# Moving columns of the fp32r matmuls taken alternately from two places 2048 bytes apart

## The chip, the cores and the metric

One core of one Trainium2 chip runs the program. The metric is the device time of one execution in microseconds, taken as the median of 3 runs.

## The reference, cut to what matters

`x` is 8 x 3072 x 256 in float32, `w_in` 256 x 2048, `w_out` 2048 x 256.

```python
X = np.fft.fft(x, axis=1)          # 3072 tokens
X = np.fft.fft(X, axis=2).real     # 256 features
h = X.reshape(8 * 3072, 256) @ w_in
g = h * np.tanh(softplus(h))       # the Mish function
out = g @ w_out
```

## The kernel before, in words

**Chunks.** The host writes the input in an order that lets symmetric tokens be added and subtracted, so that a batch (8 of them) becomes 3 chunks. A chunk has two matrices of 128 x 512, P (cosine part) and Q (sine part): its column c stands for two tokens, t and 3072 - t, whose hidden values are P-part + Q-part and P-part - Q-part. `CHUNK_TOKENS` says which token stands in which column, and `_slots` tells the host from which chunk and place of the output a token is fetched: token t from column c, its mirror from column 512 + c.

**Three-term products.** Each large product is made of three matmuls in fp32r, a type with which one matmul is one pass: a value is split into a high part, rounded to fp32r (ScalarE, `A.copy`), and the low part that is left. `split_to` (L468) does it for P and Q: ScalarE makes `ph` or `qh` (L470), VectorE or GpSimd `pl` or `ql` (L471). The matmuls of the token transform (L452 to L459) are in plain fp32, each of which appears in the trace as two records, with a weight load each. Each of the four parts of a chunk is a tile of 128 x 512 of its own, of which there are two (`new_chunk`, L463, pool `pq` with 2 buffers).

**The main loop** has 390 turns `tau`, 384 of which make a step s = tau: 8 batches x 3 chunks x 16 blocks `f` of 128 hidden units. A turn issues, in this order:

- `mm1(tau)` (L827 to L829): 6 matmuls with 512 moving columns each, 3 with `ph`, `pl`, `ph` into the PSUM tile `pa` and 3 with `qh`, `ql`, `qh` into `pb`;
- `mm2(tau - 6)` (L857): 12 matmuls with 512 moving columns each into four PSUM accumulators (2 halves of the output features x 2 halves of the 1024 token columns), from `gh` and `gl`;
- `make_h` on VectorE (L836 to L838): `h` = `pa` plus the zero-frequency row `p0b` times `wc0`, then plus `pb` into columns 0 to 511 and minus `pb` into columns 512 to 1023 of a slot of `hring`;
- `split(tau - 4)`: ScalarE casts `h` to `gh` (L846), GpSimd makes `gl` (L847; in the first 12 steps VectorE);
- the Mish activation on ScalarE (L945), in place;
- pieces of other work, given by hand: `EARLY` for the first 19 turns (conversion of the float64 weights, the first batch's sums), and after that the next batch's sums on VectorE and GpSimd (`fold_ops`, turns 10 to 44 of a batch), the transforms of `first_chunk` (turns 44 and 45), `other_chunks` (turns 1, 2, 5 and 7; in the first batch 12 to 15) and the splits of `last_chunk` (turns 17 and 18).

So 18 matmuls with 512 moving columns run in each turn, one after the other, with neighbouring columns 4 bytes apart in SBUF:

```python
T.matmul(dst, wh[:, fs], q[n + "h"], start=True, stop=False)
T.matmul(acc[i], w[:, f, 128 * d:128 * d + 128], g[:, 512 * t:512 * t + 512], **kw)
```

Before the loop, `cs` (the feature transform's table, used by `make_wc`, last in turn 10) lies in a buffer of the tag `ql`, and the small tile of `make_mids` in one of the tag `pl`. `first_p0` (L717), `col_z` (L678) and `col_cs` write the zero-frequency rows with 8 or 128 partitions. Near the end `single_h` (L900 to L902) and `single_out` (L918 to L920) compute one left-over token per batch, with 48 matmuls each; those of `single_out` have weights of only 8 columns and 256 moving columns in fp32r.

Of the kernel before, what the change touches and what calls it, by code (L numbers as in the profile page):

```python
# [10 lines left out]
F32 = mybir.dt.float32  # L11
F32R = mybir.dt.float32r
# [35 lines left out]
def _slots():  # L48

    chunk, place = np.zeros(S, np.int64), np.zeros(S, np.int64)  # L50
    for ch in range(3):
        for c, t in enumerate(CHUNK_TOKENS[ch]):
            chunk[t], place[t] = ch, c
            if t:
                chunk[S - t], place[S - t] = ch, 512 + c
    return chunk, place


# [215 lines left out]
def fft_moe(ctx, tc, x, col_d, mids_d, w_in, w_out, cs_d, dft_d, ysel_d, eye_d, out, single_d):  # L274
# [52 lines left out]
    xt = small(128, 12 * NB).rearrange("p (k c q b) -> p k c q b", k=2, c=2, q=3)  # L327
    xm = small(1, 6 * NB).rearrange("p (k q b) -> p k q b", k=2, q=3)
    eye = small(128, 128)
    cs = pqp.tile([128, 2, 2, 128], F32, tag="ql", name="cs")  # L330

    p0_d = dp.tile([NB, 3, 512], F32, name="p0_d")
    pe_d = dp.tile([NB, 1], F32, name="pe_d")
# [128 lines left out]

    def new_chunk(ch):  # L463
        q = {}
        for n in ("ph", "pl", "qh", "ql"):
            q[n] = pqp.tile([128, 512], F32R, tag=n, name=n)
        chunks[ch] = q

    def split_to(hi, lo, src, eng):
        A.copy(hi, src)  # L470
        eng.tensor_tensor(lo, src, hi, op=ALU.subtract)  # L471
# [11 lines left out]
    def first_chunk(b, par, part=(0, 1, 2)):  # L483

        ch = 3 * b
        st = folds[b]
        n = NE if par == 0 else 256
        sl = slice(256 * par, 256 * par + 256)
        if 0 in part:
            st["ps", par] = ps("pa"), ps("pb")  # L490
        pa, pb = st["ps", par]
        halves = [c for c in (0, 1) if c in part]
        transform(pa[:, :n], lambda c: fold_part(b, c, "e", 0, par), par, 0, None, halves)
        transform(pb[:, :n], lambda c: fold_part(b, c, "o", 0, par), par, 1, None, halves)
        if 2 in part:
            if par == 0:
                new_chunk(ch)
            q = chunks[ch]
            if par == 0:
                base = fp.tile([128, NE + 14], F32, tag="base", name="base")[:, :NE]  # L500
                add_mid(base, pa, 0, b)
                pa = base
            split_to(q["ph"][:, sl], q["pl"][:, sl], pa[:, :256], V)
            split_to(q["qh"][:, sl], q["ql"][:, sl], pb[:, :256], V)
            if par == 0:
                V.tensor_copy(ends[:, b:b + 1], pa[:, 256:257])

    def other_chunks(b, par, odd):

        ch = 3 * b + 1  # L510
        if par == 0 and not odd:
            new_chunk(ch)
            for o in range(2):
                full2[o] = fp.tile([128, 512], F32, tag=f"full{o}", name=f"full{o}")
        st = folds[b]
        n = NE if par == 0 else 256
        sl = slice(256 * par, 256 * par + 256)
        pa, pb = ps("pa"), ps("pb")
        y, cos, sin = ("o", 2, 1) if odd else ("e", 1, 2)
        transform(pa[:, :n], lambda c: fold_part(b, c, y, cos, par), par, 0)  # L520
        transform(pb[:, :n], lambda c: fold_part(b, c, y, sin, par), par, 1)

        base = fp.tile([128, NE + 14], F32, tag="base", name="base")[:, :NE]
        spare = fp.tile([128, 256], F32, tag="spare", name="spare")
        if par == 0:
            add_mid(base, pa, 1 + odd, b)
        else:
            V.tensor_copy(base[:, :n], pa[:, :n])

        scaled, plain = (base, pb) if odd else (pb, base)  # L530
        V.scalar_tensor_tensor(spare, scaled[:, :256], R3 if odd else -R3, plain[:, :256], op0=ALU.mult, op1=ALU.add)
        q = chunks[ch]
        h, l = ("qh", "ql") if odd else ("ph", "pl")
        split_to(q[h][:, sl], q[l][:, sl], spare, G)
        V.scalar_tensor_tensor(full2[odd][:, sl].rearrange("p (a s) -> p a s", s=128), later(scaled, par),
                               -R3 if odd else R3, later(plain, par), op0=ALU.mult, op1=ALU.add)

    def last_chunk(b, odd):

        ch = 3 * b + 2  # L540
        if not odd:
            new_chunk(ch)
        q = chunks[ch]
        h, l = ("qh", "ql") if odd else ("ph", "pl")
        split_to(q[h], q[l], full2[odd], G)

    p0b = {}

# [76 lines left out]
    sp = {}  # L625

    def make_mids():
        w = pqp.tile([128, 512], F32, tag="pl", name="mids")
        eo = w[:12 * NB, :256]
        V.tensor_tensor(eo[:, 0:128], ymid[:, 0:128], ymid[:, 128:256], op=ALU.add)  # L630
        V.tensor_tensor(eo[:, 128:256], ymid[:, 0:128], ymid[:, 128:256], op=ALU.subtract)
        n = 6 * NB
        ev, od = eo[:, 0:128], eo[:, 128:256]
        pa, pb = ps("pa"), ps("pb")
        T.matmul(pa[:n, 0:128], ysel[:, 0:n], ev, start=True, stop=True)
        T.matmul(pa[0:1, 128:128 + n], ymid[:, 256:257], ysel[:, 0:n], start=True, stop=True)
        T.matmul(pb[:n, 0:128], ysel[:, n:2 * n], od, start=True, stop=True)

        for i, (o, v) in enumerate(((n + NB, od), (n + 4 * NB, od), (3 * NB, ev))):
            T.matmul(pb[0:1, 128 * i + 128:128 * i + 256], ysel[:, o:o + 1], v, start=True, stop=True)  # L640
        m = w[:n, 256:]
        A.copy(m[:, 0:128], pa[:n, 0:128])
        A.copy(m[:, 128:256], pb[:n, 0:128])
        A.copy(xm, pa[0:1, 128:128 + n].rearrange("p (k q b) -> p k q b", k=2, q=3))
        A.copy(mid0, pb[0:1, 128:512])
        pc = psacc.tile([128, 512], F32, tag="acc0", name="pc")
        T.matmul(pc[:, 0:2 * NB], ev, ysel[:, 0:2 * NB], start=True, stop=True)
        T.matmul(pc[:, 2 * NB:3 * NB], od, ysel[:, n:n + NB], start=True, stop=True)
        A.copy(midc, pc[:, :3 * NB].rearrange("p (q b) -> p q b", b=NB))
        SP.dma_start(out=mid_d, in_=m)  # L650
# [20 lines left out]
    def col_z(par):  # L671
        n = NE if par == 0 else 256
        if par == 0:
            sp["z"] = p2.tile([128, 512], F32, tag="p0b", name="p0z")
        r = sp["z"][:NB]
        pa = ps("pa")
        transform(pa[:NB, :n], lambda c: xt[:, par, c, 0], par, 0, xm[:, 0, 0] if par == 0 else None)
        A.copy(r[:, 256 * par:256 * par + 256], pa[:NB, :256])  # L678
        if par == 0:
            A.copy(pe, pa[:NB, 256:257])  # L680
            SP.dma_start(out=pe_d, in_=pe)
            SP.dma_start(out=ends0, in_=bass.AP(pe_d.tensor, pe_d.offset, [[0, 128], [1, NB]]))
        else:
            SP.dma_start(out=p0_d[:, 0, :], in_=r)

    def col_cs(par):

        n = NE if par == 0 else 256
        if par == 0:
            sp["c"] = fp.tile([128, NE], F32, tag="full0", name="p0c")[:NB]  # L690
            sp[1] = fp.tile([128, 512], F32, tag="full1", name="p0d")[:NB]
            sp[2] = p2.tile([128, 512], F32, tag="p0b", name="p0o")[:NB]
        pa, pb = ps("pa"), ps("pb")
        transform(pa[:NB, :n], lambda c: xt[:, par, c, 1], par, 0, xm[:, 0, 1] if par == 0 else None)
        transform(pb[:NB, :n], lambda c: xt[:, 1 - par, c, 2], par, 1)
        A.copy(sp["c"][:, :n], pa[:NB, :n])
        for k in (1, 2):
            view = (lambda v: later(v, 1)) if k == 1 else (lambda v: later(v, par))
            V.scalar_tensor_tensor(later(sp[k][:, 256 * par:256 * par + 256], 1), view(pb[:NB]), R3 if k == 2 else -R3,
                                   view(sp["c"]), op0=ALU.mult, op1=ALU.add)  # L700
            if par:
                SP.dma_start(out=p0_d[:, k, :], in_=sp[k])

    def first_p0():
# [9 lines left out]
        for c in range(2):  # L714
            T.matmul(pa[:, 256:512], all_rows(xt[:, 1, c, 0]), const(c, 1, 0), start=c == 0, stop=c == 1)
        p0b[0] = p2.tile([128, 512], F32, tag="p0b", name="p0b")
        A.copy(p0b[0], pa)  # L717


    G.memset(alt, 0.0)  # L720
# [100 lines left out]
    def mm1(s):  # L821
        ch, f = divmod(s, NF)
        q = chunks[ch]
        fs = slice(128 * f, 128 * f + 128)
        pa, pb = ps("pa"), ps("pb")
        for dst, wh, wl, n in ((pa, wch, wcl, "p"), (pb, wsh, wsl, "q")):
            T.matmul(dst, wh[:, fs], q[n + "h"], start=True, stop=False)  # L827
            T.matmul(dst, wh[:, fs], q[n + "l"], start=False, stop=False)  # L828
            T.matmul(dst, wl[:, fs], q[n + "h"], start=False, stop=True)  # L829
        return pa, pb  # L830

    def make_h(s, pab):
# [16 lines left out]
    def mm2(s):  # L849
# [4 lines left out]

        def part(i, w, g, **kw):
            d, t = divmod(i, 2)
            T.matmul(acc[i], w[:, f, 128 * d:128 * d + 128], g[:, 512 * t:512 * t + 512], **kw)  # L857

        def high(i):
            part(i, woh, gh, start=f == 0, stop=False)  # L860
# [142 lines left out]
```

## Time and profile before

| | |
|---|---|
| median of 3 runs | 1746.48 us (1746.38 to 1746.68) |
| span of the profiled execution, first to last instruction | 1742.7 us |
| mean granted TensorE clock | 0.987 of full speed |
| instructions | 20578 |
| DMA, mean over the span | 39 GB/s |

The profile is of one execution. No time of its own is given for that execution beside its span; the runs' median is 3.8 us above the span, which is what lies before the first and after the last instruction. Busy time of TensorE (PE) is counted with modelled ends of pipelined matmuls, so that neighbouring matmuls overlap in it: how long a matmul really takes in a row of matmuls is read from the distance between starts. A timeline line gives the start, the duration, the engine, the line of the kernel, the operation with its output and inputs, and in brackets how long the engine was idle before it and what released it.

### The profile page before, as it was taken

How to read it: one execution, taken by the hardware profiler on the slowest of the kernel's cores; microseconds unless marked ns; L12 is line 12 of the kernel's file. 1: busy time of each engine (PE TensorE's matmuls, PEld its weight loads, DVE VectorE, ACT ScalarE, POOL GpSimd, SP SyncE). 2: the span in 40 equal slices, each digit the busy share in tenths (PEclk: the TensorE clock that was granted, in tenths of full speed). 3: DMA queues.
4: the chain of work that ended last, by engine and by line, in shares of the span. 5: the costliest groups of instructions: out<-in, count | busy, mean ns of one | idle time of the engine just before them, and what ended most of it. 6: DMA issues, size and time to landing. Idle time of an engine off the chain costs nothing.

```text
span 1742.7 us, 20578 instructions
## 1 busy us (share of the span) xinstructions
PE 1705.6 (98%) x7534; PEld 1397.0 (80%) x7534; DVE 1117.7 (64%) x1680; ACT 864.3 (50%) x968; POOL 1163.3 (67%) x654
## 2 busy tenths in 40 slices
PE   7788999999999999999999999999999999999999
PEld 4466888888888888888888888888888888888887
DVE  7997775566755666566755666556666667554453
ACT  3445454554544554455545545445544555454454
POOL 1456885687756876587756877568765777554555
PEclk8889999999999999999999999999999999998999
DMA  4212000200020000200002000100002000000000
GB/s 178 85 43 80 24 25 7 103 31 0 31 78 26 30 25 7 103 1 31 25 7 103 31 1 31 64 40 31 25 7 103 1 31 25 7 31 13 19 25 24
DMA packets 25375, 67.57 MB, mean 39 GB/s; under 512 B 3141, under 2 KB 3618, under 8 KB 25274
## 3 DMA queue, kind: packets, MB, share of 16 engines
q1 hardware_dynamic: 24474, 64.91, 10.4%
q8 instruction: 59, 0.97, 0.2%
q10 hardware_dynamic: 800, 1.35, 0.2%
q14 instruction: 42, 0.34, 0.1%
HBM read 40.97 MB, written 25.27 MB: 38 GB/s over the span
## 4 chain that ended last, share of the span: by engine, by line
PE 93%; DVE 5%; POOL 0%; issue 0%; ACT 0%; DMA 0%; ACTq 0%; DVEq 0%
PE acc L857 59%; PE pa L827 5%; PE pa L828 5%; PE pb L828 5%; PE pa L829 5%; PE pb L827 5%; PE pb L829 5%; PE pb L452 1%; PE pa L452 1%; DVE hring L836 1%; DVE gl L847 1%; DVE hring L837 1%; DVE hring L838 0%; PE pb L455 0%; DVE xring L579 0%
## 5 line engine op out<-in xcount | busy, mean ns | idle before, releaser
L847 POOL TENSOR_TENSOR gl<-hring,gh 128x1024 fp32r<-128x1024 f32 x372 | 896.7, 2411 | 475.4 <-ACT gh L846 474.8
L846 ACT CAST gh<-hring 128x1024 fp32r<-128x1024 f32 x384 | 403.1, 1050 | 733.1 <-PE acc L857 701.0
L857 PE MATMUL acc<-gh,wol 128*128 128x512 f32 x1536 | 600.8, 391 | 1.8 <-POOL wol L622 1.8
L857 PE MATMUL acc<-gh,woh 128*128 128x512 f32 x1536 | 600.9, 391 | 0.4 <-ACT woh L621 0.4
L836 DVE SCALAR_TENSOR_TENSOR hring<-p0b,wc,pa 128x512 f32<-128x512 f32 x384 | 286.5, 746 | 437.9 <-PE pa L829 422.6
L857 PE MATMUL acc<-gl,woh 128*128 128x512 f32 x1536 | 422.7, 389 | 0.0
L945 ACT ACTIVATE hring<-hring 128x1024 f32<-128x1024 f32 x384 | 404.4, 1053 | 33.4 <-DVE hring L838 24.6
L857 PEld LDWEIGHTS acc<-gh,wol 128*128 128x128 f32 x1536 | 290.3, 189 | 63.2 <-POOL wol L622 2.6
L857 PEld LDWEIGHTS acc<-gh,woh 128*128 128x128 f32 x1536 | 290.4, 189 | 61.5 <-ACT woh L621 0.9
L857 PEld LDWEIGHTS acc<-gl,woh 128*128 128x128 f32 x1536 | 289.1, 188 | 60.4
L837 DVE TENSOR_TENSOR hring<-hring,pb 128x512 f32<-128x512 f32 x384 | 264.0, 688 | 42.7 <-DVE hring L836 1.8
L838 DVE TENSOR_TENSOR hring<-hring,pb 128x512 f32<-128x512 f32 x384 | 263.8, 687 | 13.3
L827 PE MATMUL pa<-ph,wch 128*128 128x512 f32 x384 | 158.9, 414 | 9.0 <-DVE hring L836 6.8
L827 PE MATMUL pb<-qh,wsh 128*128 128x512 f32 x384 | 151.2, 394 | 4.4 <-ACT qh L470 3.3
L828 PE MATMUL pa<-pl,wch 128*128 128x512 f32 x384 | 151.0, 393 | 0.0
L828 PE MATMUL pb<-ql,wsh 128*128 128x512 f32 x384 | 150.5, 392 | 0.3 <-POOL ql L471 0.3
L829 PE MATMUL pa<-ph,wcl 128*128 128x512 f32 x384 | 150.7, 392 | 0.0
L829 PE MATMUL pb<-qh,wsl 128*128 128x512 f32 x384 | 150.6, 392 | 0.0
L827 PEld LDWEIGHTS pa<-ph,wch 128*128 128x128 f32 x384 | 72.6, 189 | 25.6 <-DVE hring L836 7.8
L827 PEld LDWEIGHTS pb<-qh,wsh 128*128 128x128 f32 x384 | 72.8, 189 | 22.1 <-ACT qh L470 3.7
L829 PEld LDWEIGHTS pa<-ph,wcl 128*128 128x128 f32 x384 | 72.9, 190 | 15.4
L828 PEld LDWEIGHTS pb<-ql,wsh 128*128 128x128 f32 x384 | 72.7, 189 | 15.8 <-POOL ql L471 0.6
(259 smaller groups left out, 1143.9 us busy)
## 6 DMA issues: line engine op xcount, KB each, us to landing
xring<-x_dram SPq DMA_DIRECT2D x32, 768.0 KB
out_dram<-ot SPq DMA_DIRECT2D x96, 256.0 KB
p0b<-p_d SPq DMA_DIRECT2D x23, 256.0 KB
wring<-w_out_dram SPq DMA_DIRECT2D x5, 512.0 KB
wring<-w_in_dram SPq DMA_DIRECT2D x3, 512.0 KB
xring<-w_in_dram SPq DMA_DIRECT2D x3, 512.0 KB
xring<-w_out_dram SPq DMA_DIRECT2D x3, 512.0 KB
wraw<-w_in_dram SPq DMA_DIRECT2D x2, 512.0 KB
```

Of the source, the lines that this page charges most:

```text
L452: T.matmul(dst, lhs(c), const(c, par, sine), start=c == 0, stop=c == 1)
L827: T.matmul(dst, wh[:, fs], q[n + "h"], start=True, stop=False)
L828: T.matmul(dst, wh[:, fs], q[n + "l"], start=False, stop=False)
L829: T.matmul(dst, wl[:, fs], q[n + "h"], start=False, stop=True)
L836: V.scalar_tensor_tensor(h[:, 0:512], p0b[ch], wc0[:, f:f + 1], pa, op0=ALU.mult, op1=ALU.add)
L837: V.tensor_tensor(h[:, 512:1024], h[:, 0:512], pb, op=ALU.add)
L838: V.tensor_tensor(h[:, 0:512], h[:, 0:512], pb, op=ALU.subtract)
L846: A.copy(gh, h)
L847: (V if s < SPLIT_V else G).tensor_tensor(gl, h, gh, op=ALU.subtract)
L857: T.matmul(acc[i], w[:, f, 128 * d:128 * d + 128], g[:, 512 * t:512 * t + 512], **kw)
L945: A.activation(hring[:, tau % RH], hring[:, tau % RH], AF.Mish)
```

## The change: what it does

The moving operand of `mm1` and `mm2` stays a set of 512 columns, but they are read in another order: column 0 of a first half, column 0 of a second half, column 1 of the first, column 1 of the second and so on, 256 from each. The two halves start 2048 bytes apart. For `gh` and `gl` these are the two halves of a row of 1024 floats. For P and Q the four tiles of a chunk become two (`h` and `l`), in which the quarters are P first half, Q first half, P second half, Q second half, so that the halves of P, and those of Q, are 2048 bytes apart. The output of a matmul is still written to 512 neighbouring columns of PSUM, in the order in which the columns were read; so `pa`, `pb`, `hring`, `gh` and the output columns are in the alternating order, and so must `p0b` be. `_slots` on the host follows it. The rows for `p0b` are written with a step of two elements (`placed`), the splits of P and Q are written to halves (`q[h][:, par]`). `cs` and the tile of `make_mids` now share a buffer of the tag `l`. Nothing is changed in the number of instructions, in their engines or in their order.

```diff
-            chunk[t], place[t] = ch, c
+            h, s = divmod(2 * (c % 256) + c // 256, 256)
+            chunk[t], place[t] = ch, 512 * h + 2 * s
             if t:
-                chunk[S - t], place[S - t] = ch, 512 + c
+                chunk[S - t], place[S - t] = ch, 512 * h + 2 * s + 1
...
-    cs = pqp.tile([128, 2, 2, 128], F32, tag="ql", name="cs")
+    early_l = pqp.tile([128, 1024], F32, tag="l", name="early")
+    cs = early_l[:, 0:512].rearrange("p (k i j) -> p k i j", k=2, i=2)
...
-        for n in ("ph", "pl", "qh", "ql"):
-            q[n] = pqp.tile([128, 512], F32R, tag=n, name=n)
+        for e in ("h", "l"):
+            both = pqp.tile([128, 1024], F32R, tag=e, name=e).rearrange("p (a k s) -> p k a s", a=2, k=2)
+            for k, n in enumerate("pq"):
+                q[n + e] = both[:, k]
...
+    def mixed(v):
+
+        return v.rearrange("p a s -> p s a")
+
+    def placed(v):
+
+        return v.rearrange("p (s a) -> p a s", a=2)
...
-            split_to(q["ph"][:, sl], q["pl"][:, sl], pa[:, :256], V)
+            split_to(q["ph"][:, par], q["pl"][:, par], pa[:, :256], V)
...
-        split_to(q[h], q[l], full2[odd], G)
+        split_to(q[h], q[l], full2[odd].rearrange("p (a s) -> p a s", a=2), G)
...
-        w = pqp.tile([128, 512], F32, tag="pl", name="mids")
+        w = early_l[:, 512:1024]
...
-        A.copy(r[:, 256 * par:256 * par + 256], pa[:NB, :256])
+        A.copy(placed(r)[:, par], pa[:NB, :256])
...
-        A.copy(p0b[0], pa)
+        A.copy(placed(p0b[0]), pa.rearrange("p (a s) -> p a s", a=2))
...
-            T.matmul(dst, wh[:, fs], q[n + "h"], start=True, stop=False)
-            T.matmul(dst, wh[:, fs], q[n + "l"], start=False, stop=False)
-            T.matmul(dst, wl[:, fs], q[n + "h"], start=False, stop=True)
+            dst = dst.rearrange("p (s a) -> p s a", a=2)
+            T.matmul(dst, wh[:, fs], mixed(q[n + "h"]), start=True, stop=False)
+            T.matmul(dst, wh[:, fs], mixed(q[n + "l"]), start=False, stop=False)
+            T.matmul(dst, wl[:, fs], mixed(q[n + "h"]), start=False, stop=True)
...
-            T.matmul(acc[i], w[:, f, 128 * d:128 * d + 128], g[:, 512 * t:512 * t + 512], **kw)
+            T.matmul(acc[i].rearrange("p (s a) -> p s a", a=2), w[:, f, 128 * d:128 * d + 128],
+                     mixed(g.rearrange("p (a s) -> p a s", a=2)[:, :, 256 * t:256 * t + 256]), **kw)
```

## Rows read from the trace of the kernel before

**Rows 1.** The page, part 1: busy us of each engine, share, instructions.

```profile
PE 1705.6 (98%) x7534; PEld 1397.0 (80%) x7534; DVE 1117.7 (64%) x1680; ACT 864.3 (50%) x968; POOL 1163.3 (67%) x654
```

**Rows 2.** The page, part 4: the chain that ended last, by engine.

```profile
PE 93%; DVE 5%; POOL 0%; issue 0%; ACT 0%; DMA 0%; ACTq 0%; DVEq 0%
```

**Rows 3.** Stages: length; busy PE, PEld, DVE, ACT, POOL; clock; DMA share; GB/s.

```profile
90.00:163.00 73.00, 60.39 (x235) 45.94 (x234) 63.75 (x95) 35.19 (x49) 36.16 (x32) 0.91 0.20 69
163.00:1596.00 1433.00, 1432.54 (x6409) 1190.48 (x6409) 915.49 (x1353) 729.83 (x790) 1024.61 (x565) 1.00 0.09 33
```

**Rows 4.** Timeline of PE, one turn of the loop, and the start of the next.

```profile
1614.99 0.39 PE L827 MATMUL pa<-ph,wch 128*128 128x512 f32 x1
...
1619.07 0.39 PE L827 MATMUL pa<-ph,wch 128*128 128x512 f32 x1
```

**Rows 5.** Timeline of PE just after `single_h`, 8 matmuls at the low clock.

```profile
1605.14 0.63 PE L828 MATMUL pa<-pl,wch 128*128 128x512 f32 x1
...
1608.55 0.63 PE L857 MATMUL acc<-gh,woh 128*128 128x512 f32 x1
```

**Rows 6.** Timeline of PE in `single_out`, first and last of 30 matmuls.

```profile
1625.22 0.28 PE L918 MATMUL pa<-woh,endgh 128*8 128x256 f32 x1
...
1628.51 0.28 PE L920 MATMUL pa<-woh,endgl 128*8 128x256 f32 x1
```

**Rows 7.** Timeline of PE in a plain fp32 transform, first and fourth pair of records.

```profile
703.38 0.59 PE L452 MATMUL pa<-dft,F0e 128*128 128x256 f32 x2
...
704.67 0.59 PE L452 MATMUL pb<-dft,F1e 128*128 128x256 f32 x2
```

**Rows 8.** The chain in order of time: two sets of six plain fp32 records.

```profile
11.60 2.58 PE pa L751 x6
14.18 2.59 PE pb L751 x6
```

**Rows 9.** PE groups by line, 152.7 us to the end: busy, mean ns, idle.

```profile
L857 PE MATMUL acc<-gh,woh 128*128 128x512 f32 x1492 | 581.0, 389 | 0.0
L857 PE MATMUL acc<-gh,wol 128*128 128x512 f32 x1492 | 580.9, 389 | 0.5 <-POOL wol L622 0.5
L857 PE MATMUL acc<-gl,woh 128*128 128x512 f32 x1493 | 411.0, 389 | 0.0
L827 PE MATMUL pa<-ph,wch 128*128 128x512 f32 x367 | 149.0, 406 | 0.0
L828 PE MATMUL pa<-pl,wch 128*128 128x512 f32 x367 | 143.2, 390 | 0.0
L827 PE MATMUL pb<-qh,wsh 128*128 128x512 f32 x367 | 143.2, 390 | 0.0
L829 PE MATMUL pa<-ph,wcl 128*128 128x512 f32 x367 | 143.2, 390 | 0.0
L829 PE MATMUL pb<-qh,wsl 128*128 128x512 f32 x367 | 143.1, 390 | 0.0
L828 PE MATMUL pb<-ql,wsh 128*128 128x512 f32 x367 | 143.0, 390 | 0.0
```

**Rows 10.** The ten turns in which POOL has most to do, as in rows 3.

```profile
768.50:809.30 40.80, 40.80 (x181) 33.80 (x181) 27.81 (x40) 22.29 (x25) 34.15 (x22) 1.00 0.10 33
```

**Rows 11.** Timeline, turn 16: the first use of the second chunk.

```profile
142.59 0.58 PE L827 MATMUL pa<-ph,wch 128*128 128x512 f32 x1
...
146.91 0.49 PE L827 MATMUL pb<-qh,wsh 128*128 128x512 f32 x1 [3.27 <-ACT qh L470]
```

**Rows 12.** Instructions of single lines: duration in ns, least/median/most, first and last start.

```profile
L717 ACT COPY p0b<-p x1: 585/585/585, 22.1 to 22.1; 128x512 f32<-128x512 f32 x1
...
L584 DVE SCALAR_TENSOR_TENSOR wu<-xring,wu x6: 681/684/694, 65.2 to 132.8; 128x512 int32<-128x512 int32 x6
...
L837 DVE TENSOR_TENSOR hring<-hring,pb x384: 686/687/690, 35.6 to 1720.2; 128x512 f32<-128x512 f32 x192
```

More of the change, by code (lines that the diff above doesn't have):

```diff
@@ L487, in first_chunk @@
         n = NE if par == 0 else 256
-        sl = slice(256 * par, 256 * par + 256)
         if 0 in part:
@@ L502, in first_chunk @@
                 pa = base
-            split_to(q["ph"][:, sl], q["pl"][:, sl], pa[:, :256], V)
-            split_to(q["qh"][:, sl], q["ql"][:, sl], pb[:, :256], V)
+            split_to(q["ph"][:, par], q["pl"][:, par], pa[:, :256], V)
+            split_to(q["qh"][:, par], q["ql"][:, par], pb[:, :256], V)
             if par == 0:
@@ L533, in other_chunks @@
         h, l = ("qh", "ql") if odd else ("ph", "pl")
-        split_to(q[h][:, sl], q[l][:, sl], spare, G)
+        split_to(q[h][:, par], q[l][:, par], spare, G)
         V.scalar_tensor_tensor(full2[odd][:, sl].rearrange("p (a s) -> p a s", s=128), later(scaled, par),
@@ L698, in col_cs @@
             view = (lambda v: later(v, 1)) if k == 1 else (lambda v: later(v, par))
-            V.scalar_tensor_tensor(later(sp[k][:, 256 * par:256 * par + 256], 1), view(pb[:NB]), R3 if k == 2 else -R3,
+            V.scalar_tensor_tensor(later(placed(sp[k])[:, par], 1), view(pb[:NB]), R3 if k == 2 else -R3,
                                    view(sp["c"]), op0=ALU.mult, op1=ALU.add)
```

## The prediction

> **What bounds the kernel now.** I read the page's busy shares first: TensorE is busy for 98% of the span, GpSimd for 67%, VectorE for 64% [rows 1]. A busy share alone does not make a bound, so the chain that ended last came next: 93% of it is TensorE, 5% VectorE [rows 2]. The stages say where the 5% lie: from 90 to 163 us TensorE is busy for 60.4 of 73 us and VectorE for 63.8, at a mean clock of 0.91; from 163 to 1596 us TensorE is busy for 1432.5 of 1433 us at full clock [rows 3]. The large matmuls have next to no idle time before them in any group from 152.7 us on [rows 9]. So nine tenths of the time are one unbroken row of matmuls, and what counts is the distance between their starts, since their busy times overlap.
>
> A turn of the loop takes 1619.07 - 1614.99 = 4.08 us for 18 matmuls, 226.7 ns each [rows 4]. [...]
>
> [...]
> [...]
> [...]
>
> [...]
>
> **The change part by part.**
>
> *The order of the columns* is the only thing that changes in the steady loop. Rows 9 count 1492 + 1492 + 1493 + 6 x 367 = 6679 such matmuls after 152.7 us; about 11 run at the low clock behind `single_h` [rows 5], which leaves 6668. No row shows a moving operand read from two places, so the price is bounded from both sides. At best nothing is lost: 213.3 ns, a gain of 13.4 x 6668 = 89 us. At worst each column costs two cycles, as at the low clock: 426.3 ns [rows 5], a loss of 199.6 x 6668 = 1331 us. [...] Saved: 226.7 - 215.8 = 10.9 ns x 6668 = 72.7 us.
>
> [...]
>
> *The first 152.7 us* hold 234 more such matmuls (3 x 1536 + 6 x 384 = 6912 in all; one is cut by the window of rows 9), but VectorE sets their pace [rows 3]. At most they give 10.9 x 234 = 2.6 us; I count nothing.
>
> *The shared tile.* Where a tile is waited for as a whole, P's matmuls would also wait for Q's parts. From batch 1 on Q is written 9 turns or more ahead (turn 7 for 16, turns 44 and 45 for 48, turn 18 for 32). In turn 16 P's three matmuls ran from 142.59 and Q's waited until 146.91 [rows 11]; behind Q's parts P's three (0.7 us) would come after that wait, and the same in turn 0. Cost: nothing to 1.5 us, I take nothing. The buffers change hands no earlier than before: a chunk's buffer was last read one turn or more before its next writer is issued, and `cs` for the last time in turn 10, two turns before its buffer is wanted.
>
> *Strided writes and split rows.* The copy to `p0b` took 0.585 us at 22.1 us and its first reader is the L836 just ahead of the first L837 at 35.6 us [rows 12]; twice as long would still be hidden. VectorE with an input at every second word took 684 ns for 512 columns and 687 without [rows 12], so I count nothing for strides there, nor for the splits. The `col_z` and `col_cs` writes are a handful with 8 partitions. Nothing is moved in any queue, no DMA is added.
>
> *What is late next.* With 18 x 215.8 ns a turn is 3.88 us. In the ten turns in which GpSimd has most to do it is busy for 34.15 of 40.8 us [rows 10]; ten shorter turns are 38.8 us, so 88%, still under. VectorE (27.8 us there) has more room. So TensorE stays the bound and the whole gain shows.
>
> **The sum** against the profiled span: 1742.7 - 72.7 = 1670.0 us; the runs' median stands 3.8 us above the span, so 1673.8 us.
>
> **The rivals.**
>
> - *Slower: every column pays for the change of place.* Now neighbouring columns come from neighbouring addresses, and afterwards no two in succession do. If a read brings several neighbouring columns at once, alternating throws that away. It decides from a distance of 227.2 ns on (0.5 ns x 6668 is 0.2% of the time). [...] Worked out with two cycles per column as in rows 5: 1746.5 + 1331 = 3077 us. [...] I give this rival 2 in 10.
> - *No change: the loss is not one of addresses.* [...] This is also the case in which the change doesn't do what it says, the two streams being fetched as before. [...] Time: 1746.5 us, 1.5 more if the shared tile's waits show. 1.5 in 10.
>
> **How the numbers follow.** The forecast has 6.5 in 10: 1673.8 us, in its own range 1657 (213.3 ns, 1746.5 - 89) to 1711 (half of the gain lost to a partial cure or to late buffers, 1746.5 - 36). No change and the slower rival hold 1.5 and 2. The range takes in the forecast and no change with its waits, 1657 to 1751, and leaves the slower case out. About 0.2% (3.5 us) is what a measurement of this kernel can tell from no change. Faster by more than that 0.65, within it 0.15, slower 0.20.
>
> **What would show it right or wrong.** Right: the turn of rows 4 takes 3.88 us, `single_out` (which is not changed) keeps its 113.4 ns, the low-clock distances stay at 426, and GpSimd's share rises to about 70% of the span. Wrong: a turn of 4.08 us (no change), a turn of over 4.09, up to 7.7 us (each column pays), or idle time before L827 and L857 on `gl`, `ph` or `qh`, which would mean that the matmuls became shorter and something else took the gain.

## The result, and the profile after

The changed kernel takes 1674.3 us (median of 4 runs, 1672.6 to 1674.7) against 1746.6 us before (4 runs, 1746.4 to 1747.3). The ratio is 0.9585, with a 95% interval of 0.9572 to 0.9599. The forecast was 1673.8 us.

The page of the changed kernel, parts 1 and 4, answers to [rows 1, 2]:

```profile
PE 1630.5 (97%) x7534; PEld 1403.6 (84%) x7534; DVE 1122.9 (67%) x1680; ACT 862.7 (52%) x968; POOL 1153.5 (69%) x654
...
PE 92%; DVE 6%; POOL 1%; issue 0%; DMA 0%; ACT 0%; DVEq 0%; ACTq 0%; POOLq 0%
```

TensorE is still the bound: the same 7534 records, and the chain is still nine tenths TensorE. The page counts 20901 instructions in all where it counted 20578, which the section on the change did not foresee: TensorE's queue has 324 more semaphore instructions, which do not count as busy. The first experiment below has them too, and its turn is as long as before. What became shorter is the distance between matmuls. The timeline of PE, one turn of the loop and the start of the next, as in [rows 4]:

```profile
752.84 0.38 PE L839 MATMUL pa<-h,wch 128*128 128x512 f32 x1
...
756.72 0.38 PE L839 MATMUL pa<-h,wch 128*128 128x512 f32 x1
```

A turn takes 3.88 us where it took 4.08, so 215.6 ns for each of 18 matmuls by these rounded times; over 20 turns it is 215.8. Two more stretches of PE's timeline show what did not move: seven matmuls at the low clock behind `single_h`, as in [rows 5], and 27 of `single_out`, which still reads neighbouring columns, as in [rows 6]:

```profile
1541.40 0.63 PE L840 MATMUL pa<-l,wch 128*128 128x512 f32 x1
...
1543.96 0.63 PE L869 MATMUL acc<-gh,wol 128*128 128x512 f32 x1
...
1559.00 0.28 PE L931 MATMUL pa<-woh,endgh 128*8 128x256 f32 x1
...
1561.96 0.28 PE L933 MATMUL pa<-woh,endgl 128*8 128x256 f32 x1
```

Behind `single_h` the granted clock is 0.50 in both profiled executions (windows from 1605.14 to 1608.55 us before and from 1541.40 to 1544.00 in the changed kernel), and six distances take 2.56 us, 426.7 ns each, against 426.3 before. Half of 426.7 is 213.3 ns: that is an estimate, from this clock and this distance, of 512 columns at full clock at the rate they have at 0.50. The 226.7 ns of [rows 4] are 13.4 above it, one sixteenth, and 215.8 are 2.5 above it. In `single_out` 26 distances take 2.96 us, 113.8 ns each against 113.4 before, which is half of 226.7 for half the columns: the sixteenth is still lost where the order is the old one, in the same execution in which the large matmuls lost it no more.

The stages, with length, then busy us of PE, PEld, DVE, ACT and POOL with their counts, the clock, the DMA share and GB/s, answer to [rows 3, 10]:

```profile
90.00:163.00 73.00, 57.02 (x225) 43.19 (x224) 63.32 (x91) 34.14 (x47) 34.42 (x30) 0.91 0.19 69
163.00:1525.00 1362.00, 1360.53 (x6384) 1193.37 (x6383) 915.33 (x1349) 724.76 (x786) 1009.66 (x563) 1.00 0.10 35
...
744.80:783.60 38.80, 38.80 (x181) 33.97 (x181) 28.36 (x40) 22.19 (x25) 33.78 (x21) 1.00 0.10 35
```

From 163 us on TensorE has next to no gap: it is idle for 1.5 of 1362 us, against 0.5 of 1433 before. In the ten turns with most work for GpSimd that engine is busy for 33.78 of 38.8 us, 87%: it got fuller and took nothing back. The first 163 us gained nothing. VectorE sets the pace there: of the 132 us of the chain between 31 and 163 us it has 83 before and 87 in the changed kernel. Turn 20 begins at these times in the two profiled executions (timeline of PE, kernel before and changed kernel):

```profile
164.87 0.39 PE L827 MATMUL pa<-ph,wch 128*128 128x512 f32 x1
```

```profile
167.87 0.38 PE L839 MATMUL pa<-h,wch 128*128 128x512 f32 x1
```

From there to the end the kernel before needs 1742.7 - 164.9 = 1577.8 us and the changed one 1672.6 - 167.9 = 1504.7: 73.1 us less, of which the first part of this one execution lost 3.0. Turn 20 began at 164.9 to 167.7 us in five executions that read this part in the old order, and at 166.3 to 167.9 us in three that read it in the new one (the others are runs of the experiments below), so those 3 us are of the size by which executions differ in their first part. From turn 20 to the end they agree: 1577.8 and 1577.9 us in the old order, 1504.6 to 1504.8 in the new.

Not all of the 73.1 us come from the distance at full clock. From amid the 48 matmuls of `single_h` on, which have 8 moving columns each, a clock of 0.50 was granted for 10.2 us before and for 6.8 us in the changed kernel. Turns 356 and 357 of the loop, which lie there, became 1.93 us shorter, where 36 distances account for 0.39; so some 1.5 us are the clock's, which the prediction did not count. 25 us around that place, before and after, in the columns of the stages:

```profile
1590.00:1615.00 25.00, 25.00 (x115) 21.84 (x114) 10.27 (x18) 8.49 (x11) 9.75 (x5) 0.80 0.11 43
```

```profile
1529.00:1554.00 25.00, 25.00 (x126) 22.45 (x125) 11.66 (x20) 9.69 (x12) 10.95 (x6) 0.86 0.11 43
```

### The profile page after: what moved, and what is told of

It is laid out like the page before. It is cut to its first block, busy times and chain, and to the rows that moved or that the text cites. A ratio compares the mean times of both kernels' runs of the same rounds, so it can differ in the third digit from the quotient of the medians.

```text
span 1672.6 us, 20901 instructions
## 1 busy us (share of the span) xinstructions
PE 1630.5 (97%) x7534; PEld 1403.6 (84%) x7534; DVE 1122.9 (67%) x1680; ACT 862.7 (52%) x968; POOL 1153.5 (69%) x654
## 4 chain that ended last, share of the span: by engine, by line
PE 92%; DVE 6%; POOL 1%; issue 0%; DMA 0%; ACT 0%; DVEq 0%; ACTq 0%; POOLq 0%
PE acc L869 58%; PE pa L839 5%; PE pb L840 5%; PE pa L840 5%; PE pb L839 5%; PE pb L841 5%; PE pa L841 5%; PE pa L454 1%; PE pb L454 1%; DVE gl L859 1%; DVE hring L848 1%; DVE hring L849 1%; DVE wu L595 0%; DVE wu L589 0%; DMA hring<-table_ysel_dram 0%
## 5 line engine op out<-in xcount | busy, mean ns | idle before, releaser
L839 PE MATMUL pa<-h,wch 128*128 128x512 f32 x384 | 155.4, 405 | 7.2 <-DVE hring L848 5.0
L839 PE MATMUL pb<-h,wsh 128*128 128x512 f32 x384 | 147.2, 383 | 5.2 <-ACT h L482 3.5
L840 PE MATMUL pb<-l,wsh 128*128 128x512 f32 x384 | 146.7, 382 | 0.3 <-POOL l L483 0.3
L840 PE MATMUL pa<-l,wch 128*128 128x512 f32 x384 | 146.8, 382 | 0.0
L841 PE MATMUL pb<-h,wsl 128*128 128x512 f32 x384 | 146.6, 382 | 0.0
L841 PE MATMUL pa<-h,wcl 128*128 128x512 f32 x384 | 146.6, 382 | 0.0
L839 PEld LDWEIGHTS pa<-h,wch 128*128 128x128 f32 x384 | 73.3, 191 | 20.1 <-DVE hring L848 5.6
L839 PEld LDWEIGHTS pb<-h,wsh 128*128 128x128 f32 x384 | 73.1, 190 | 18.3 <-ACT h L482 3.9
L840 PEld LDWEIGHTS pb<-l,wsh 128*128 128x128 f32 x384 | 73.2, 191 | 11.1 <-POOL l L483 0.6
L841 PEld LDWEIGHTS pa<-h,wcl 128*128 128x128 f32 x384 | 73.4, 191 | 10.6
```

Source lines behind the costliest of these rows:

```text
L839: T.matmul(dst, wh[:, fs], mixed(q[n + "h"]), start=True, stop=False)
L840: T.matmul(dst, wh[:, fs], mixed(q[n + "l"]), start=False, stop=False)
L841: T.matmul(dst, wl[:, fs], mixed(q[n + "h"]), start=False, stop=True)
```

## The experiments

Two theories stood at the start. Theory 1: the order of reading gives the gain, because an address must not lie next to the one just read. The rival: the gain comes from where the tiles lie. In the second round theory 1 had a rival of another kind, theory 2, which came out of the first round.

**The layout without the order.** The shared tiles stay, the order of reading goes back:

```diff
-        return v.rearrange("p a s -> p s a")
+        return v
...
-            dst = dst.rearrange("p (s a) -> p s a", a=2)
+            dst = dst.rearrange("p (a s) -> p a s", a=2)
...
+            T.matmul(acc[i], w[:, f, 128 * d:128 * d + 128], g[:, 512 * t:512 * t + 512], **kw)
```

> The changed kernel with its shared tiles, but with the 512 columns of each matmul read from neighbouring addresses again, and output columns and zero-frequency rows in the old order. Theory 1 (the order of reading is what gave the gain): distance between matmuls back at 226.7 ns, a turn of 4.08 us, 1746.5 us within 2. Rival (the gain comes from where the tiles lie or from fewer, larger tiles): distance 215.8 ns, about 1674 us.

Measured: 1745.9 us against 1746.6 before, ratio 0.9999 (0.9989 to 1.0008). The timeline of PE, one turn and the start of the next:

```profile
780.04 0.39 PE L838 MATMUL pa<-h,wch 128*128 128x512 f32 x1
...
784.12 0.39 PE L838 MATMUL pa<-h,wch 128*128 128x512 f32 x1
```

The turn is back at 4.08 us. The whole gain is the order's; the shared tile by itself gives nothing and costs nothing, within 2 us.

**The order in mm2 alone.** mm1 reads neighbours, mm2 as in the changed kernel:

```diff
-        return v.rearrange("p a s -> p s a")
+        return v
...
-            dst = dst.rearrange("p (s a) -> p s a", a=2)
+            dst = dst.rearrange("p (a s) -> p a s", a=2)
...
-                     mixed(g.rearrange("p (a s) -> p a s", a=2)[:, :, 256 * t:256 * t + 256]), **kw)
+                     g.rearrange("p (a s) -> p a s", a=2)[:, :, 256 * t:256 * t + 256].rearrange("p a s -> p s a"), **kw)
```

> The changed kernel with the alternating order in mm2 alone (12 of 18 matmuls of a turn); mm1 reads neighbouring columns. Theory 1, each matmul being paid by itself: mm1 at 226.7 ns, mm2 at 215.8, a turn of 6 x 226.7 + 12 x 215.8 = 3.95 us, so two thirds of the gain: 1746.5 - 72.3 x 2/3 = 1698 us. Rival (the loss sits in something shared by neighbouring matmuls, so that one kind alone cures or spoils all): 1674 or 1746 us.

Measured: 1706.5 us, ratio 0.9774 (0.9760 to 0.9789). The timeline of PE, where a turn begins, where its mm2 begins, and where the next turn begins:

```profile
763.84 0.40 PE L839 MATMUL pa<-h,wch 128*128 128x512 f32 x1
...
765.24 0.38 PE L869 MATMUL acc<-gh,woh 128*128 128x512 f32 x1
...
767.82 0.40 PE L839 MATMUL pa<-h,wch 128*128 128x512 f32 x1
```

The 12 matmuls of mm2 take 2.58 us, 215.0 ns each by these rounded times, so they are cured by themselves ("cured" stands below for 215.8 ns instead of 226.7). The 6 of mm1 take 1.40 us, 233 ns each (231.8 by the finer times of the trace), and not 226.7. So the gain was 40 us where two thirds would be 48. Both expectations missed: a matmul is mostly paid by itself, but the six that read neighbours cost some 5 ns more each behind and between cured ones than among their like.

**Which distance.** Each batch reads its 512 columns in another order, two places in turn at a distance `d` (in elements of 4 bytes). In the pattern each pair is a step and a count, and the last pair runs fastest:

```diff
+            m = bass.AP(row.tensor, row.offset + o, [list(row.ap[0]), [1, 256], [d, 2]])
+            return dst.rearrange("p (s a) -> p s a", a=2), m
...
+            o, m = taken(acc[i], g, ch // 3, t)
+            T.matmul(o, w[:, f, 128 * d:128 * d + 128], m, **kw)
```

> Each batch reads its 512 moving columns in another order, in mm1 and mm2 alike (the products are then of other columns, so the output holds other values; the work is the same). Batch 0: neighbouring columns; batches 1 to 7: two places in turn, at distances of 1024, 512, 256, 128, 64, 16 and 2048 bytes. Read from the distance between starts in each batch. Theory 1a (any two places do, each place then having twice the time): 215.8 ns in all of batches 1 to 7. Theory 1b (the distance matters, the two places must fall into different parts of the memory): 215.8 at 2048, 226.7 or more at some of the shorter ones. [...]

This kernel and the next two ran once each, so what is read of them is the distance between starts, in turns at full clock (the mean granted clock of the three executions is 0.987, 0.991 and 0.989). Measured: a turn of 3.885 us, 215.8 ns per matmul, in all of batches 1 to 7, that is at 1024, 512, 256, 128, 64, 16 and 2048 bytes, and 226.7 ns between the neighbours of batch 0. A turn and the start of the next at 1024 bytes and at 16 bytes:

```profile
370.31 0.38 PE L861 MATMUL pa<-h,wch 128*128 128x512 f32 x1
...
374.19 0.38 PE L861 MATMUL pa<-h,wch 128*128 128x512 f32 x1
...
1342.02 0.38 PE L861 MATMUL pa<-h,wch 128*128 128x512 f32 x1
...
1345.91 0.38 PE L861 MATMUL pa<-h,wch 128*128 128x512 f32 x1
```

The 2048 bytes are nothing special. That fits theory 1a and rules 1b out.

**Other distances, steps and runs.** The same kernel with other entries; "step" takes one place with a step, "run" takes runs of neighbours from two places in turn:

```diff
+            m = bass.AP(row.tensor, row.offset + 256 * k, [list(row.ap[0]), [d, 256 // d], [512, 2], [1, d]])
...
+            m = bass.AP(row.tensor, row.offset, [list(row.ap[0]), [1, 512 // n], [d, n]])
```

> As the run before, with other orders by batch. 0: neighbouring columns; 1: two places 3072 bytes apart; 2: 2112 bytes; 3: 2056 bytes; 4: 1536 bytes; 5: one place, every second column (a step of 8 bytes over 4096 bytes); 6: two neighbours from each of two places 2048 bytes apart; 7: sixteen neighbours from each of two places 2048 bytes apart. Theory 1a: 215.8 in batches 1 to 4; 226.7 or between in 5 (one place, but no address next to the last) and in 6 and 7 more of the loss the longer the run of neighbours. Theory 1b (parts of the memory chosen by the address): 1 to 4 differ among each other; 7 near 226.7.

Measured: 215.8 ns at 3072, 2112 and 1536 bytes, 216.7 at 2056. But every second column of one place took 451 ns, twice the time, where theory 1 expected 226.7 at most; pairs took 328 and runs of sixteen 240, both slower than plain neighbours. A turn and the start of the next, for the step of 8 bytes and for the pairs:

```profile
1212.96 0.63 PE L861 MATMUL pa<-h,wch 128*128 128x512 f32 x1
...
1221.08 0.63 PE L861 MATMUL pa<-h,wch 128*128 128x512 f32 x1
...
1581.40 0.51 PE L861 MATMUL pa<-h,wch 128*128 128x512 f32 x1
...
1587.31 0.51 PE L861 MATMUL pa<-h,wch 128*128 128x512 f32 x1
```

8.12 us by 18 are 451 ns, 5.91 by 18 are 328. With the step no address lies next to the one before, and it is the slowest. Theory 1 fell here. Theory 2 took its place: what counts is the step from a column to the next but one, as if odd and even columns were fetched as two strands. In the changed order each strand walks over neighbours (4 bytes), in the old order it takes steps of 8, with a step of two columns steps of 16, and with pairs it jumps to the other place at each read. For these the measured distances are 215.8, 226.7, 451 and 328 ns.

**Orders that part the two theories,** one for each chunk of 16 turns, the pattern of mm1 first and that of mm2 behind it:

```diff
+        (((1, 128), (256, 4)), ((1, 128), (256, 4))),
+        (((1, 256), (0, 2)), ((1, 256), (0, 2))),
+        (((2, 256), (512, 2)), ((2, 256), (512, 2))),
+        (((0, 2), (4, 128), (512, 2)), ((0, 2), (4, 128), (512, 2))),
+        (((1, 256), (1, 2)), ((1, 256), (1, 2))),
...
+            m = bass.AP(row.tensor, row.offset, [list(row.ap[0])] + [list(x) for x in order])
```

> Each chunk of 16 turns reads its 512 moving columns in another order (other columns are then multiplied, the work is the same); read from the distance between starts. Theory 1 (rest: an address must not lie next to the one just read; any change of place helps). [...] Four places in turn, 1024 bytes apart: theory 1 215.8 ns, theory 2 over 300, as with pairs (328). Each column twice: theory 1 over 226, theory 2 215.8. Two places 2048 bytes apart, each with a step of 8 bytes: theory 1 215.8, theory 2 226.7. The same with a step of 16 bytes: theory 1 215.8, theory 2 about 451. Two places 4 and 8 bytes apart: theory 1 over 226, theory 2 215.8. Runs of 4 and 8 neighbours from each of two places: both between 240 and 328, falling. Eight places in turn: theory 1 215.8, theory 2 as four places. One place with a step of 16 bytes: both 451 or more. Two places 2052 and 2056 bytes apart: both 216 to 217. Alternating in mm1 alone, in mm2 alone: neighbours beside cured matmuls at 231, as measured before.

Measured, a turn and the start of the next in the timeline of PE: four places in turn; each column twice; two places with a step of 8 bytes each; two places with a step of 16 bytes each; two places 4 bytes apart:

```profile
329.04 0.45 PE L882 MATMUL pa<-h,wch 128*128 128x512 f32 x1
...
334.14 0.45 PE L882 MATMUL pa<-h,wch 128*128 128x512 f32 x1
...
396.75 0.38 PE L882 MATMUL pa<-h,wch 128*128 128x512 f32 x1
...
400.63 0.38 PE L882 MATMUL pa<-h,wch 128*128 128x512 f32 x1
...
459.68 0.39 PE L882 MATMUL pa<-h,wch 128*128 128x512 f32 x1
...
463.76 0.39 PE L882 MATMUL pa<-h,wch 128*128 128x512 f32 x1
...
561.45 0.63 PE L882 MATMUL pa<-h,wch 128*128 128x512 f32 x1
...
569.57 0.63 PE L882 MATMUL pa<-h,wch 128*128 128x512 f32 x1
...
662.48 0.38 PE L882 MATMUL pa<-h,wch 128*128 128x512 f32 x1
...
666.36 0.38 PE L882 MATMUL pa<-h,wch 128*128 128x512 f32 x1
```

These are turns of 5.10, 3.88, 4.08, 8.12 and 3.88 us, by 18 matmuls 283, 216, 227, 451 and 216 ns. In all five theory 1 expected another value, and in four of them theory 2 expected these: reading the same address twice in succession costs no more than two places in turn (215.8 ns), and two places far apart cost as much as plain neighbours as soon as each is walked in steps of 8 bytes, and twice the time with steps of 16. The form of the pattern is not what cures: two places with steps of 4 and of 8 bytes have the same form and differ by 11 ns. Four places in turn came out a little under what theory 2 had (over 300). All orders together, by the distance between starts, in turns in which mm1 and mm2 both have the order (mm2 runs six turns behind):

| order of the columns | step to the next but one | ns per matmul |
|---|---|---|
| two places in turn, 4 to 3072 bytes apart; each column twice | 4 bytes | 215.8 (216.7 at 8 and 2056 bytes) |
| neighbours; two places, each with a step of 8 bytes | 8 bytes | 226.7 |
| one place, step of 8 bytes; two places, step of 16 each | 16 bytes | 451 |
| one place, step of 16 bytes | 32 bytes | 461 |
| runs of 16, 8 and 4 neighbours from each of two places | 8 bytes within a run, then far | 240, 243, 250 |
| pairs of neighbours from each of two places | far each time | 328 to 333 |
| four places in turn, 1024 bytes apart | far each time | 283 |
| eight places in turn, 512 bytes apart | far each time | 487 |

Theory 2 did not foresee that eight places would be so much slower than four (a turn of 8.76 us, the first two lines below). Nor does the step to the next but one settle the cost by itself: four places, pairs and eight places all take a strand far away at each read, and cost 283, 328 and 487 ns, the first two less than a step of 16 bytes.

Alternating in mm2 alone gave 215.8 ns there and 232 for the neighbours in mm1, as expected. Alternating in mm1 alone did not cost the expected 231: a turn takes 4.02 us, which is the sum of its parts (6 x 215.8 + 12 x 226.7 ns) but for 5 ns. Only the first neighbours' matmul behind the cured ones is slower, some 232 ns; the other eleven keep 226.7. The last four lines are the start of such a turn, its first two matmuls of mm2 and the start of the next turn:

```profile
1452.58 0.67 PE L882 MATMUL pa<-h,wch 128*128 128x512 f32 x1
...
1461.34 0.67 PE L882 MATMUL pa<-h,wch 128*128 128x512 f32 x1
...
1069.23 0.38 PE L882 MATMUL pa<-h,wch 128*128 128x512 f32 x1
...
1070.52 0.40 PE L911 MATMUL acc<-gh,woh 128*128 128x512 f32 x1
1070.75 0.39 PE L911 MATMUL acc<-gh,wol 128*128 128x512 f32 x1
...
1073.25 0.38 PE L882 MATMUL pa<-h,wch 128*128 128x512 f32 x1
```

**The order without the shared tile.** The kernel before, with its four tiles per chunk, and P's and Q's halves 1024 bytes apart in their own tiles:

```diff
+    def mixed(v):
+
+        return v.rearrange("p (a s) -> p s a", a=2)
...
+            dst = dst.rearrange("p (s a) -> p s a", a=2)
+            T.matmul(dst, wh[:, fs], mixed(q[n + "h"]), start=True, stop=False)
```

> The kernel before with the alternating order and without the shared tiles: P and Q keep four tiles, their halves are 1024 bytes apart, those of gh and gl 2048. Both theories: 215.8 ns in all 18 matmuls, a turn of 3.885 us, 1674 us within 2, the same as the changed kernel. Rival (the distance of 2048 bytes or the shared tile is needed in the complete kernel): up to 1698 us, mm1 not being cured.

The changed kernel on the same chip:

> The changed kernel once more, on the same chip as the run with own tiles: 1674 us, the same as that one within 0.1%.

Measured: own tiles 1672.6 us, ratio to before (1744.8 us on this chip) 0.9585 (0.9572 to 0.9599); the changed kernel 1674.4 us, 0.9597 (0.9584 to 0.9610). The intervals overlap, the turn of the loop is the same in both, and so is the time from turn 20 to the end (1504.6 and 1504.8 us); with own tiles:

```profile
752.29 0.38 PE L837 MATMUL pa<-ph,wch 128*128 128x512 f32 x1
...
756.17 0.38 PE L837 MATMUL pa<-ph,wch 128*128 128x512 f32 x1
```

So the shared tile can be left out. The 1.8 us between the medians, just over the 0.1% expected, are not shown to be a difference.

## Why the prediction was right, and where its reason was not

- *The bound and the count.* Right: one unbroken row of matmuls after the first 163 us, and the gain is the distance times their number. From turn 20 on 73.1 us were gained, some 1.5 of them by the clock; the sum had 72.7 for a stretch that begins three turns earlier. The 3.8 us between span and time were misread: in every execution for which both are known the time is 1.8 us above the span (1674.39 and 1672.6 for the profiled one here), so the profiled execution before was some 2 us faster than the median. The span after is 1672.6 us where the sum has 1670.0; the time forecast, the median before less 72.7 us, is not touched by it.
- *The distance after.* Right to a tenth of a nanosecond, which is partly luck: the 215.8 ns of the sum was the author's estimate, and no run of the kernel before shows it, nor the 213.3 of the range. What the runs show in their place is 215.8 ns in the alternating order at full clock, and 426.7 at a clock of 0.50, half of which is 213.3. What the 2.5 ns between the two are is not shown: no matmul of another length was run in the alternating order.
- *What kind of loss it is.* Right in the signs that were named for it: `single_out`, which is not changed, keeps its distance (113.8 ns, 113.4 before), and so do the matmuls at the low clock (426.7 ns, 426.3 before). The loss goes with the columns, 113.4 ns for 256 [rows 6] and 226.7 for 512 [rows 4]. At a clock of 0.50 it is gone: there both orders take 426 to 427 ns. At full clock it comes and goes with the order of reading alone (226.7 and 215.8 ns, first experiment).
- *Why alternating should cure it.* The reason that stands with theory 1a, "each place then having twice the time", is wrong. Each column read twice leaves no time and takes 215.8 ns; four places leave four times and take 283. In orders of one or two places the step that counts is that from a column to the next but one: 4 bytes now, 8 before. The number came out because both reasons give the same for this one order. That is luck: by theory 1a's reason four places would have been as good a choice, and by the measured distance they would have cost some 377 us (56.6 ns x 6668, an estimate) instead of gaining 72.
- *The rival that every column pays.* In the changed kernel all 512 columns change the place, 2048 bytes away, and the matmul takes 215.8 ns, less than the 226.7 of neighbours. Nor was the rival's price the worst: 426.3 ns was set as that, and every second column of one place takes 451, eight places in turn 487. A strand that goes far away at each read has no single price here: pairs and four places take 328 and 283 ns.
- *The distance of 2048 bytes.* The prediction did not say whether it mattered; it does not, from 4 bytes to 3072, but for 0.8 ns at 8 and 2056 bytes.
- *The covered edits.* Right: GpSimd went to 87% in its fullest ten turns (88 forecast) and to 69% of the span (about 70). The shared tile's wait did not come: in turn 16 Q's matmuls waited, but P's had started 4.5 us ahead of them, as in [rows 11]. The timeline of PE in the changed kernel:

```profile
146.11 0.57 PE L839 MATMUL pa<-h,wch 128*128 128x512 f32 x1
...
150.60 0.48 PE L839 MATMUL pb<-h,wsh 128*128 128x512 f32 x1 [3.49 <-ACT h L482]
```

What stays open: whether there are two strands in the chip or something that acts like them; why four places cost 283 ns and eight 487, and pairs 328; why the six neighbours' matmuls of mm1 cost 232 ns among cured ones, while of the twelve of mm2 only the first is slower; why the low clock at `single_h` lasted less long in the new order.

## What to carry to other kernels

Where fp32r matmuls with 512 columns, one record each in the trace, stand in an unbroken row and the distance between their starts is 226.7 ns at full clock, let the columns come from two places in turn, so that every second column is the neighbour of the last but one: 215.8 ns, one twentieth of the matmul time, for an order that the host can undo. Any two of the places tried do (4 to 3072 bytes apart: 215.8 ns, 216.7 at 8 and 2056 bytes), the halves of one tile of 512 included; four or eight places (283 and 487 ns), pairs and longer runs from two places (328 to 333 and 240 to 250), or a step of two columns in one place (451) are worse than plain order, by up to a little over twice the time. Only fp32r with 512 columns was tried, and only at full clock was there anything to gain (at a granted clock of 0.50 the old order took 426.3 ns and the alternating one 426.7). Take the order over everywhere: with plain mm1 among alternating mm2 a sixth of the gain that was due was lost. Judge such a loss by the distance between starts in other places too (here 113.4 ns with 256 columns, 426.3 with 512 at a clock of 0.50) before looking for waits: the busy share of 98% said nothing of it.

## What the runs showed of the hardware that had not been expected

- In orders of one or two places the cost of a moving fp32r column (4 bytes, full clock) goes with its distance from the column two before it: 4 bytes 215.8 ns per 512 columns, 8 bytes 226.7, 16 bytes 451, 32 bytes 461. Where that distance is far at each column, it does not tell the cost: four places 283, pairs 328 to 333, eight places 487.
- Reading the same column twice in succession costs no more than reading two columns of two places (215.8 ns).
- A change of place at each column, 4 to 3072 bytes away, takes 215.8 ns with two places (216.7 at 8 and 2056 bytes), less than the 226.7 of neighbours, 283 ns with four and 487 with eight.
- Six fp32r matmuls in plain order take 232 ns each between twelve in the alternating order, so that two thirds of the change gave 40 of 72 us; of twelve in plain order behind six alternating ones only the first is slower (232 ns).
